# Attention: which ring of buffers keeps a wait between score matmuls and the evictions of turned queries and keys

## The chip, the cores and the metric

The kernel runs on one core of a Trainium2 chip. The metric is the device time of one execution in microseconds. PE is the matrix engine, ACT the scalar engine, DVE the vector engine, POOL the general engine, SP the engine that issues most transfers. PEld is PE's loading of weights, the operand that stays in the array. A wait is a semaphore value that an instruction's engine must see before the instruction may start; every engine takes its instructions in order, so what stands behind a waiting instruction waits too.

## What is computed

Attention with a threshold, then a feed-forward network with a squared ReLU, all of it in fp32 values (the weights of the network arrive as 64-bit floats and are converted on the chip).

```python
# q, k, v: (8, 8, 576, 64); w_in: (512, 2048); w_out: (2048, 512)
scores = q @ k.transpose(0, 1, 3, 2) / 8
scores = np.where(scores >= scores.max(-1, keepdims=True) - tau, scores, -1e9)
attn = np.exp(scores - scores.max(-1, keepdims=True))
attn = attn / (attn.sum(-1, keepdims=True) + 1e-9)
x = (attn @ v).transpose(0, 2, 1, 3).reshape(4608, 512)
h = np.maximum(x @ w_in, 0.0)
out = h * h @ w_out
```

## The kernel before

**Tiling.** Two heads of a batch element form a pair; there are 32 pairs. A pair's 576 queries are four blocks of 128 (`FULL`) and a rest of 64 (`REST`). A unit is what goes through the softmax at once: one block of 128 queries of one pair, or the two rests of two neighbouring pairs. So two pairs make nine units, eight with t < FULL and one with t = FULL, and there are 144 units. A period works on two units, A (even) and B (odd), so there are 72 periods and a few more to drain the pipeline. The unit with t = FULL is unit A of periods 4, 13, 22, ... and unit B of periods 8, 17, 26, ....

**Order.** The order of the work in a period is written out by hand, in `PLAIN`, `CONVERTING` (periods in which a chunk of the weights is converted, up to period 34) and `BEGIN_WITH`. Each name is a step: SA and SB the scores of unit A and B, T the transposes of a pair's queries or keys into PSUM (line 398), eT their eviction to SBUF by ACT (lines 403 and 411), top the maxima (DVE, line 452), pow the exponentials (ACT, line 462), mask the threshold (DVE, line 467), U, V and W the transposes of the weights of attention (lines 380 and 515), eU, eV and eW their evictions (ACT, line 523), PV the products with the values (line 532), x their eviction. `TURNS` sets the periods in which a pair's queries or keys are turned: one such turn in eight of nine periods. Query turns that matter below: pair 19 in period 39, pair 20 in period 42.

**PSUM.** One tile `sc` holds six banks. The main scores (64 x 512) of unit A are written to banks 0 and 5, those of unit B to banks 2 and 3. The small scores of both units (64 x 64, against the last 64 keys) and the turned queries and keys share banks 1 and 4. W uses banks 2 and 3, the values banks 0 and 5.

**SBUF rings.** A turned pair has three tiles (`places`, line 332): qT, the 512 queries of its full blocks, in a ring of `Q_RING` = 3 buffers; kT, its 576 keys, and qR, its 64 rest queries, in rings of `K_RING` = 4. A block unit's scores read qT and kT of its pair; the unit with t = FULL reads qR and kT of two pairs, and no qT.

**Waits.** The framework sees `sc` as one tile, and so sees a dependence between any two instructions that write and read it. `touch` (line 355) goes over the earlier instructions on other engines: where the banks are the same it adds the wait for the last of each engine, and where they are not it takes the framework's dependence away, except for the pairs of kinds in `MEET`, when the two pair numbers differ by a multiple of one of the rings given there. Those are kept, because the tiles in SBUF may be the same buffer. The kinds are "scores" (line 437) and "turned" (lines 403 and 411), with either ring.

Of the kernel before, what the change touches and what calls it, by code (L numbers as in the profile page):

```python
# [14 lines left out]
AF = mybir.ActivationFunctionType  # L15
# [33 lines left out]
def kernel(  # L49
# [25 lines left out]
    nc = tc.nc  # L75
# [5 lines left out]
    FULL = S // P  # L81
# [3 lines left out]
    BANK = 512  # L85
# [25 lines left out]
    qscale = const.tile([P, 1], FP32, name="qscale")  # L111
# [160 lines left out]
    loaded, loaded_v, turned, weights = {}, {}, {}, {}  # L272
# [59 lines left out]
    def places(i):  # L332
        if i not in turned:
            turned[i] = (
                sb.tile([P, MAIN], FP32, tag="qT", bufs=Q_RING, name="qT"),
                sb.tile([P, S], FP32, tag="kT", bufs=K_RING, name="kT"),
                sb.tile([P, REST], FP32, tag="qR", bufs=K_RING, name="qR"),
            )
        return turned[i]
# [3 lines left out]
    def ask_ahead(i, which):  # L343

        while asked[which] < min(len(pairs) - 1, i + (2 if i else 1)):
            asked[which] += 1
            (load_k if which else load_q)(asked[which])
# [2 lines left out]
    behind = mybir.DependencyInfo(mybir.DependencyClass.Sync, mybir.DependencyReason.DATA)  # L350

    Q_RING, K_RING, W_RING = 3, 4, 2
    MEET = (("scores", "turned", (Q_RING, K_RING)), ("values", "weights", (W_RING,)), ("x", "weights", (W_RING,)))

    def touch(what, made, at, size, key=0):

        if at is None:
            return
        on = range(at // BANK, (at + size - 1) // BANK + 1)
        met = {made.ins.engine}  # L360
        for kind, other, others, its in reversed(touched):
            e = other.ins.engine
            if e == made.ins.engine:
                continue
            if on[-1] < others[0] or others[-1] < on[0]:
                if any({what, kind} == {x, y} and any((key - its) % n == 0 for n in rings) for x, y, rings in MEET):
                    continue
                tc.declare_no_dep(made.ins, other.ins, reason="other banks")
            elif e not in met:
                met.add(e)  # L370
                tc.add_manual_dep(made.ins, other.ins.name, behind, reason="same bank")
        touched.append((what, made, on, key))
        while len(touched) > 300:
            touched.popleft()
# [16 lines left out]
    def turn(i, which, spots, other=None):  # L391

        nat, to = loaded.pop((i, which)), places(i)
        of = [nat[:, t, :] for t in range(FULL)] + ([loaded.pop((i, 2))] if which else [])
        for t, x in enumerate(of):
            for r, (spot, at) in enumerate(spots):
                rows = ds(r * HALF, HALF)
                made = nc.tensor.transpose(spot[:, ts(t, HALF)], x[rows, :], ident[rows, rows])  # L398
                touch("turns", made, at, BANK)
        half = FULL * HALF  # L400

        def scaled(to, spot):
            touch("turned", nc.scalar.activation(out=to, in_=spot[0], func=AF.Identity, scale=qscale[:, :]), spot[1], BANK, i)  # L403

        def then():
            part = lambda r, x, n: (spots[r][0][:, ds(x, n)], spots[r][1])
            if which:
                for r, n in ((0, half), (1, half + REST)):
                    spot = part(r, 0, n)
                    copy_by = other if r and other else nc.scalar.copy  # L410
                    touch("turned", copy_by(to[1][:, ds(r * half, n)], spot[0]), spot[1], BANK, i)
                scaled(to[2], part(0, half, REST))
                ask_ahead(i, 1)
            else:
                for r in range(2):
                    scaled(to[0][:, ds(r * half, half)], part(r, 0, half))
                ask_ahead(i, 0)

        return then
# [3 lines left out]
    def scores(n, rest):  # L423

        of, t = units[n]
        at_k, count = (MAIN, REST) if rest else (0, MAIN)
        for j in range(2):
            first = n % 2 != j
            to = (3 * j + 1) * BANK + first * (BANK - REST) if rest else (3 * j + 2 * first) * BANK
            for c in range(2):  # L430
                rows, at = ds(j * D, D), ds(c * HALF, HALF)
                qT, kT, qR = turned[of[c]]
                lhs = qT[rows, ds((c * FULL + t) * HALF, HALF)] if t < FULL else qR[rows, :]
                made = nc.tensor.matmul(  # L434
                    sc[at, ds(to, count)], lhs, kT[rows, ds(at_k, count)], start=True, stop=True
                )
                touch("scores", made, to, count, of[c])

    def softmax(n):

# [47 lines left out]
    for g in range(2, 2 * len(pairs)):  # L488
        two, x = divmod(g - 4, 4)
# [129 lines left out]
    def period(p):  # L619
# [19 lines left out]
        def turn_some():  # L639
            free = None  # L640
            if turns and p < 2:
                pq = pt_pool.tile([P, 2, BANK], FP32, tag="pt", name="pq")
                free = [(pq[:, r, :], None) for r in range(2)]
            late["turn"] = [turn(g // 2, g % 2, free or spots()) for g in turns]
# [30 lines left out]
        def scored_a():  # L675
            if has(A):
                scores(A, False)
                scores(A, True)
                scores(B_, True)
                softmax(A)  # L680
# [336 lines left out]
    with tc.manual_schedule():  # L1017
        with ExitStack() as stack:
# [18 lines left out]
            keep_busy(15)  # L1037
            pq = pt_pool.tile([P, 2, BANK], FP32, tag="pt", name="pq")
            turn(0, 0, [(pq[:, r, :], None) for r in range(2)])()
            keep_busy(8, sc[:, ds(5 * BANK, P)])  # L1040
            turn(0, 1, spots(), nc.vector.tensor_copy)()
            for i in range(1, 3):
                load_v(i)
# [88 lines left out]
        for n in range(NSTEP):  # L1132
            last = n == NSTEP - 1
# [105 lines left out]
```

## Time and profile before

| what | value |
|---|---|
| median of 3 runs | 1302.54 us (1302.05, 1302.54, 1305.91) |
| the profiled execution's own time | 1302.09 us |
| its span | 1300.3 us |
| busy PE / DVE / ACT / POOL | 1280.6 / 1009.3 / 846.5 / 916.7 us |
| attention, about 0 to 506 us | PE, DVE and ACT in turn on the chain |
| hidden layer, 506 to about 900 us | PE |
| output layer, about 900 us to the end | PE |
| line 434 (scores) on PE | 176.5 us, 2304 records |
| line 403 (scaled evictions) on ACT | 96 instructions, 0.46 us for 128x256 |

How to read it: the profile gives for each group of instructions the busy time, and the idle time of the engine just before them with what ended it. A fp32 matmul of this kernel is two or more records. The timeline merges neighbouring instructions of one line: start, length, engine, line, operation, count, and in brackets the idle time before and what ended it; the end of a matmul is modelled, so that a merged row of PE can reach a little into the next. Stretches of time are compared by the start of a line's rows.

### The profile page before, as it was taken

What the parts mean: (1) busy time and instruction counts of PE and PEld (TensorE: products, weight loads), DVE (VectorE), ACT (ScalarE), POOL (GpSimd) and SP (SyncE); (2) the same over time, 40 slices, a digit from 0 to 9 for tenths busy, and PEclk for the clock granted to TensorE, in tenths of its full rate; (3) what the DMA queues carried; (4) which work ended last, traced back from release to release, by engine and by line L of the source; (5) the groups of instructions that cost most, each with busy time, mean ns of one, the idle gap of its engine ahead of it and who ended that gap; (6) DMA issues with size and microseconds to landing.
All of it is one profiled execution on the core that took longest, in us unless ns stands there. A gap on an engine that the chain in (4) does not pass through costs nothing.

```text
span 1300.3 us, 47830 instructions
## 1 busy us (share of the span) xinstructions
PE 1280.6 (98%) x19463; PEld 1157.1 (89%) x19463; DVE 1009.3 (78%) x2431; ACT 846.5 (65%) x1498; POOL 916.7 (71%) x1023
## 2 busy tenths in 40 slices
PE   8999999999999999999999999999999999999998
PEld 5777777777777778999999999999999999999998
DVE  6999999999999995877787778777646654665463
ACT  6999999989998984757675766575523432343240
POOL 2787787755555321977897879768777767777775
PEclk9999999999999999999999999999999999999999
DMA  6656666544333312556655765579645224522411
GB/s 154 168 144 156 161 186 183 142 106 110 82 87 78 89 33 67 164 182 222 200 166 186 227 195 164 163 280 390 218 158 163 85 84 159 162 77 91 159 34 34
DMA packets 247035, 192.12 MB, mean 148 GB/s; under 512 B 97184, under 2 KB 195488, under 8 KB 246816
## 3 DMA queue, kind: packets, MB, share of 16 engines
q1 hardware_dynamic: 245504, 188.66, 48.5%
q8 instruction: 153, 2.51, 0.8%
q14 instruction: 66, 0.54, 0.1%
q10 hardware_dynamic: 1312, 0.41, 0.1%
HBM read 116.65 MB, written 72.35 MB: 145 GB/s over the span
## 4 chain that ended last, share of the span: by engine, by line
PE 91%; ACT 4%; DVE 3%; DMA 2%; issue 1%; POOL 0%; ACTq 0%; POOLq 0%; SPq 0%; DVEq 0%
PE ph L840 30%; PE po L975 29%; PE sc L532 11%; PE sc L434 10%; PE pt L380 6%; DVE arena L452 2%; PE sc L515 2%; PE sc L398 2%; ACT arena L523 1%; ACT arena L462 1%; DMA wall<-w 1%; PE sc L380 1%; DMA g<-arena 0%; ACT arena L403 0%; PE idle L1027 0%
## 5 line engine op out<-in xcount | busy, mean ns | idle before, releaser
L125 POOL TENSOR_TENSOR arena<-arena 128x512 f32<-128x512 f32 (+1 forms) x314 | 377.7, 1222 | 133.3 <-DVE arena L125 115.2
L975 PE MATMUL po<-wall,arena 128*128 128x128 f32 x3528 | 394.9, 275 | 1.4 <-ACT arena L752 1.4
L975 PEld LDWEIGHTS po<-wall,arena 128*128 128x128 f32 x3528 | 394.3, 192 | 2.0 <-ACT arena L752 1.8
L840 PE MATMUL ph<-arena,wall 128*128 128x128 f32 x3528 | 394.2, 275 | 0.7 <-DVE arena L659 0.7
L840 PEld LDWEIGHTS ph<-arena,wall 128*128 128x128 f32 x3528 | 394.0, 192 | 0.8 <-issue 0.8
L125 DVE TENSOR_TENSOR arena<-ph,arena 128x512 f32<-128x512 f32 x378 | 256.4, 689 | 86.2 <-PE ph L840 66.3
L122 POOL TENSOR_TENSOR arena<-arena 128x128 f32<-128x128 f32 (+2 forms) x314 | 254.7, 812 | 50.2 <-DMA arena<-w 33.8
L125 DVE TENSOR_TENSOR arena<-po,arena 128x128 f32<-128x128 f32 x378 | 108.3, 290 | 167.9 <-PE po L975 163.7
L467 DVE SCALAR_TENSOR_TENSOR arena<-arena 128x576 f32<-128x576 f32 x288 | 235.4, 853 | 0.7 <-ACT arena L462 0.7
L462 ACT ACTIVATE arena<-arena 128x576 f32<-128x576 f32 x288 | 208.6, 773 | 7.5 <-DVE arena L452 4.2
L452 DVE TENSOR_SCALAR_CACHE_REDUCE arena<-sc 128x576 f32<-128x576 f32 x288 | 205.2, 748 | 10.4 <-ACT arena L523 4.2
L786 ACT COPY c<-arena 128x512 f32<-128x512 f32 (+1 forms) x303 | 173.5, 579 | 50.1 <-DVE arena L122 41.3
L532 PEld LDWEIGHTS sc<-arena 64*64 64x64 f32 x5760 | 158.8, 133 | 35.6 <-DVE arena L452 19.4
L532 PE MATMUL sc<-arena 64*64 64x128 f32 (+1 forms) x5760 | 179.3, 262 | 2.7 <-DVE arena L452 1.5
L434 PE MATMUL sc<-arena 64*64 64x64 f32 (+1 forms) x2304 | 176.5, 414 | 3.4 <-ACT arena L403 2.3
L122 DVE TENSOR_TENSOR arena<-arena,c 128x512 f32<-128x512 f32 (+1 forms) x267 | 174.9, 663 | 5.9 <-ACT c L786 4.0
L523 ACT COPY arena<-pt 128x1024 f32<-128x1024 f32 x144 | 146.4, 1017 | 27.5 <-PE pt L380 26.3
L752 ACT COPY arena<-po 128x128 f32<-128x128 f32 x63 | 16.7, 264 | 186.5 <-PE po L975 183.7
L380 PEld LDWEIGHTS pt<-ident,arena 64*128 64x128 f32 x2304 | 83.4, 139 | 40.4 <-ACT arena L523 29.3
L752 ACT COPY arena<-ph 128x512 f32<-128x512 f32 x63 | 36.6, 582 | 124.3 <-PE ph L840 123.8
L434 PEld LDWEIGHTS sc<-arena 64*64 64x64 f32 x2304 | 74.2, 134 | 41.4 <-issue 14.4
L380 PE MATMUL pt<-ident,arena 64*128 64x64 f32 x2304 | 102.3, 229 | 3.6 <-ACT arena L523 2.2
(51 smaller groups left out, 918.7 us busy)
## 6 DMA issues: line engine op xcount, KB each, us to landing
g<-arena SPq DMA_DIRECT2D x144, 256.0 KB, 2.4
arena<-g SPq DMA_DIRECT2D x144, 256.0 KB, 4.6
w<-arena SPq DMA_DIRECT2D x60, 256.0 KB, 2.4
wall<-w SPq DMA_DIRECT2D x49, 256.0 KB, 5.2
arena<-w SPq DMA_DIRECT2D x44, 256.0 KB, 3.4
arena<-in_v_dram SPq DMA_DIRECT2D x32, 288.0 KB, 4.0
out_dram<-arena SPq DMA_DIRECT2D x70, 128.0 KB, 2.3
arena<-in_q_dram SPq DMA_DIRECT2D x64, 128.0 KB, 3.9
```

The lines of the kernel that those rows point to most:

```text
L122: e.tensor_tensor(out=out, in0=x, in1=y, op=ALU.subtract)
L125: e.tensor_tensor(out=out, in0=x, in1=y, op=ALU.add)
L380: made = nc.tensor.transpose(pt[:, r, ts(slot, HALF)], of[rows, :], ident[rows, rows])
L434: made = nc.tensor.matmul(sc[at, ds(to, count)], lhs, kT[rows, ds(at_k, count)], start=True, stop=True)
L452: made = nc.vector.tensor_scalar(out=s[:, j, :], in0=sc[:, ds(at, S)], scalar1=1.0, scalar2=None, op0=ALU.mult, op1=ALU.min, accum_out=nmx ...
L462: nc.scalar.activation(out=w[:, :, j, :], in_=of(j), func=AF.Exp, bias=nmx[:, j : j + 1], scale=-1.0)
L467: nc.vector.scalar_tensor_tensor(out=w[:, :, j, :], in0=of(j), scalar=thr[:, j : j + 1], in1=w[:, :, j, :], op0=ALU.is_le, op1=ALU.mult, a ...
L523: touch("weights", nc.scalar.copy(joined(to), whole(pt, 0, count)), at, 2 * BANK, m)
L532: made = nc.tensor.matmul(sc[ds(u * D, D), ds(5 * j * BANK + row, count)], loaded_v[i][rows, (c - (u != j)) % CH, :], wT[m][rows, ds(weigh ...
L786: nc.scalar.copy(c, y)
L840: nc.tensor.matmul(to[:, j, :], W_IN[m, k][:, ts(j, P)], of[k][:, m - 1, :], start=(not more and j == 0), stop=True, skip_group_check=True,)
L975: nc.tensor.matmul(to, g[:, j, :], w[:, j, :], start=(not more and j == 0), stop=(j == 3), skip_group_check=True)
```

## The change

`MEET` gets a row for each combination that shares a buffer: block scores ("scores") with queries ("q turned") in the ring of 3, block scores with keys and rest queries ("k turned") in the ring of 4, and the scores of the unit with t = FULL ("last scores") with "k turned" alone. The kind of an eviction is taken from `which` (1 for the turn of keys and rest queries), that of a score from t.

```diff
-    MEET = (("scores", "turned", (Q_RING, K_RING)), ("values", "weights", (W_RING,)), ("x", "weights", (W_RING,)))
+    MEET = (
+        ("scores", "q turned", (Q_RING,)), ("scores", "k turned", (K_RING,)), ("last scores", "k turned", (K_RING,)),
+        ("values", "weights", (W_RING,)), ("x", "weights", (W_RING,)),
+    )
...
         half = FULL * HALF
+        kind = "k turned" if which else "q turned"
...
-            touch("turned", nc.scalar.activation(out=to, in_=spot[0], func=AF.Identity, scale=qscale[:, :]), spot[1], BANK, i)
+            touch(kind, nc.scalar.activation(out=to, in_=spot[0], func=AF.Identity, scale=qscale[:, :]), spot[1], BANK, i)
...
-                    touch("turned", copy_by(to[1][:, ds(r * half, n)], spot[0]), spot[1], BANK, i)
+                    touch(kind, copy_by(to[1][:, ds(r * half, n)], spot[0]), spot[1], BANK, i)
...
-                touch("scores", made, to, count, of[c])
+                touch("scores" if t < FULL else "last scores", made, to, count, of[c])
```

## Prediction

> **What bounds the kernel now.** I read first the busy shares by stretch, to find the stage that the change touches. The columns are the stretch, its length, then the busy time and number of records of each engine, the granted clock, the DMA share and GB/s.
>
> ```profile
> 14.00:256.00 242.00, 235.32 (x5764) 175.91 (x5763) 240.12 (x647) 231.32 (x414) 185.47 (x230) 0.99 0.63 166
> 256.00:500.00 244.00, 240.16 (x6358) 181.31 (x6358) 233.83 (x704) 217.31 (x335) 118.40 (x170) 1.00 0.35 81
> 506.00:911.00 405.00, 404.44 (x3619) 404.26 (x3620) 311.00 (x493) 260.10 (x469) 320.49 (x372) 1.00 0.64 209
> ```
>
> Attention takes the first 500 us. In its first half (the weights are converted beside it) VectorE leaves 1.9 us of 242 idle and PE 6.7. In the second half PE leaves 3.8 us idle in 244 and VectorE 10.2. From 506 us on the feed-forward layers keep PE full, and no line of the change acts there. So the change is worth what it takes out of attention.
>
> Second, line 403, the eviction whose waits the change edits on ScalarE, over the whole run (us, times):
>
> ```profile
> L403 ACT ACTIVATE arena<-sc,qscale x91: 314/455/474, 7.4 to 471.2; 128x256 f32<-128x256 f32 x60, 128x64 f32<-128x64 f32 x31
> ...
> its engine sat idle before it (us, times) until:
>   DVE tau_p L119: 0.8, 1
> ```
>
> ScalarE has once stood idle before this line, for 0.8 us at the start, and never for PE. Third, line 434, the score matmuls, in the second half alone (256 to 480 us):
>
> ```profile
> L434 PE MATMUL sc<-arena x1092: 216/589/641, 255.6 to 479.7; 64*64 64x512 f32 x91, 64*64 64x64 f32 x91
> its engine sat idle before it (us, times) until:
>   ACT arena L403: 1.6, 4
> ```
>
> PE stands before the scores for line 403 four times, 1.6 us in sum, and for nothing else there. Fourth, the timeline at the first of these, PE and then ScalarE:
>
> ```profile
> 285.89 0.46 PE L515 MATMUL sc<-ident,arena 64*64 64x64 f32 x16
> 286.75 1.32 PE L434 MATMUL sc<-arena 64*64 64x512 f32 x24 [0.41 <-ACT arena L403]
> 288.00 0.52 PE L398 MATMUL sc<-ident,arena 64*128 64x64 f32 x10
> ...
> 285.89 0.81 ACT L403 ACTIVATE arena<-sc,qscale 128x256 f32<-128x256 f32 x2
> 286.60 1.00 ACT L523 COPY arena<-pt 128x1024 f32<-128x1024 f32 x1
> ```
>
> The scores start 0.05 us after the second eviction ends (285.89 + 0.81 = 286.70). The same picture, with 0.41, 0.41 and 0.42 us, stands at 345.90, 405.02 and 464.45.
>
> **The change, part by part.** The instructions of both programs, engine by engine, are the same ones in the same order; eleven waits differ.
>
> (a) Seven query evictions (line 403, periods 8, 17, 26, 35, 44, 53, 62) no longer wait for the last of the 64-row score matmuls. Cost and gain 0: by the second view ScalarE never stood there for PE. In those periods powers (line 462) lie before the eviction on ScalarE, and each waits for a maximum that reads the same group's scores. If that cover were gone, at most one 64x512 pass (0.59 us by the median of the mixed row above) would show per site, 4 us in all, and that would be a gain. I take 0, because the row that measures it shows none.
>
> (b) At the four sites above (periods 40, 49, 58, 67) the four main matmuls of the 64-row unit lose their wait for the query evictions. There the unit's first pair and the evicted pair differ by 3 (pair 16 and pair 19), which is a hit in the ring of 3, though these matmuls read no tile of that ring. The third small matmul of the group now waits for the second eviction, the first for the first one: they write the banks that the evictions read, so these waits are real.
>
> What a site is worth I take from a period that has the same evictions and not the wait, period 43, ahead of which pair 20's queries are evicted (that unit belongs to pair 19, which differs by 1):
>
> ```profile
> 306.00 0.46 PE L515 MATMUL sc<-ident,arena 64*64 64x64 f32 x16
> 306.28 1.27 PE L434 MATMUL sc<-arena 64*64 64x512 f32 x24
> 307.48 0.53 PE L398 MATMUL sc<-ident,arena 64*128 64x64 f32 x10
> ...
> 305.77 0.82 ACT L403 ACTIVATE arena<-sc,qscale 128x256 f32<-128x256 f32 x2
> ```
>
> From the start of line 515: scores at +0.28, transposes (line 398) at +1.48, and, further on in that timeline, the next filling of pt at +1.84, the second scores at +2.44, the values at +3.35, the next line 515 at +6.52 (312.52). At the site: +0.86, +2.11, +2.48, +3.07, +3.98, +7.15 (293.04). From the transposes on the difference is 0.63 us at every step. It is larger than the idle 0.41 because the first scores overlap the tail of line 515 when they need not wait (0.17 us more), and the group itself is 0.05 shorter. So a site is worth 0.63 us, bounded from below by the idle alone, 0.41, and from above by the 0.72 us that VectorE idles there (below).
>
> Is the wait only moved to the small matmuls? If the main ones start at 285.89 + 0.28 = 286.17, they run 0.91 us (the second scores of the period before, 281.87, to the values, 282.78), to 287.08. The second eviction has ended at 286.70. Cover 0.38 us; the two new waits cost 0, and in period 43 the weight loads show a wait of 0.28 us for line 403 in this very place and PE none. Without the cover they would cost the whole gain.
>
> What is late next, with everything 0.63 us earlier, at the first site: the filling of pt would come at 287.74, and the copy that frees it (line 523) ends at 287.60: 0.14 us left. The second scores at 288.33 need the copy of the middle banks, which ends at 288.09: 0.24 left. VectorE's first maximum:
>
> ```profile
> 288.65 0.76 DVE L452 TENSOR_SCALAR_CACHE_REDUCE arena<-sc 128x576 f32<-128x576 f32 x1 [0.72 <-ACT arena L523]
> ```
>
> It stands 0.72 us behind the mask before it, which ends at 287.92. The copy named had ended at 288.09, so the last to come is PE's transposes in the same bank (288.00 + 0.52). Moved to 288.02 it keeps 0.1 us of idle. All later steps hang on these, so the 0.63 us is carried on. POOL waits 2.6 us each period for VectorE and has no backlog there.
>
> One wait fewer on the first matmul also takes away an extra instruction of PE's queue:
>
> ```profile
> L434 PEldq EVENT_SEMAPHORE  x1: 51/51/51, 285.9 to 285.9; - x1
> ```
>
> It lies in the idle before 286.75 and is worth 0 by itself. The Trainium skill (Perfetto Trace Analysis, "Identifying Dependency Chains") says that an instruction that waits for several engines may get EventSemaphore instructions ahead of it; the trace agrees, and counted as a gain of its own that would be 4 x 0.051 = 0.2 us more, a time of 1299.8.
>
> The sum: 4 x 0.63 = 2.5 us. The profiled execution took 1302.09 with a span of 1300.3: the span becomes 1297.8, that execution 1299.6. It lies 0.45 us under the median of the runs shown (1302.54), so I forecast 1302.54 - 2.5 = **1300.0**, 0.19% less. Own range: 4 x 0.41 = 1.6 gives 1300.9, 4 x 0.72 = 2.9 gives 1299.7, widened to 1298.5 to 1301.5 for the scatter of a median (the two lower runs lie 0.5 us apart, the highest 3.4 above them).
>
> **The rivals.** *Absorbed* (1302.5): VectorE is 96% busy in the second half (233.83 of 244), so PE's time could be off the path that sets the end. Against it: VectorE idles 0.71 to 0.72 us at all four sites, right behind PE's stall, and the period behind the first site makes up at most 0.2 us of the stall (6.34 us from line 515 to line 515, 293.04 to 299.38, in a period that turns nothing; period 43 took 6.52 and turns keys). It also covers the change not doing what it says, the stall coming back at the small matmuls (cover 0.38).
>
> *More* (1290.6 to 1295.3): weight loads before line 434 wait 11.6 us for line 403 in 256 to 480, 29 times. Four of them (0.55 each, 2.2 us) are the sites; if the other 9.4 us were false waits as well and all on the path, the time would be 1302.5 - 2.5 - 9.4 = 1290.6; half of it on the path gives 1295.3. Against it: the programs differ in no other wait, and PE stands at none of the 25.
>
> *Slower* (1305.2): behind the hidden layer the chain runs through one queue of transfers, four in a row at 890 to 911 us.
>
> ```profile
> 896.21 5.07 DMA wall<-w
> 901.35 5.15 DMA g<-arena
> ```
>
> If the shift put one more store (5.15 us) ahead of a weight's reload there, it would cost 5.2 - 2.5 = 2.7 us over before. It decides only if a transfer of that stage is timed by something other than the stage itself. Against it: these loads and stores are issued behind semaphores of the same stage, which starts 2.5 us earlier as a whole.
>
> **How the numbers follow.** Forecast 79%, absorbed 12%, more 5%, slower 4%. I call 0.3% (3.9 us) what a measurement of this kernel can tell from no change: faster means under 1298.6. Forecast and absorbed lie inside it but for the scatter of a median: 10 points of the forecast's 79 may fall under 1298.6. Faster 0.05 + 0.10 = 0.15; slower 0.04; same 0.81. The range 1297.8 to 1302.8 takes in the forecast's own range, the absorbed case and some of the scatter; it leaves out the case of more, the slower one, and about 5 points of scatter.
>
> **What would show it.** In the profile after: no PE wait for line 403 before the scores between 256 and 480 us; at each site line 515 to the transposes 1.48 us in place of 2.11; VectorE's 0.72 us before the first maximum down to about 0.1; the feed-forward part starts at 503.5 in place of 506.0 and takes as long as before; the first half ends where it did. It is wrong if the scores start early and the transposes don't, if the period behind a site grows by what was won, or if the start of the feed-forward part moves by under 1.6 or over 2.9 us.

## The result and the profile after

Over 13 executions each the changed kernel took 1301.14 us (median, 1298.72 to 1304.56), the kernel before 1303.27 us (1301.62 to 1305.91). The ratio is 0.9983, 95% interval [0.9975, 0.9991]: 0.17% faster, some 2.2 us, and so less than the 0.3% set out above. The profiled execution has a span of 1298.3 us against 1300.3.

The first view again, busy time by stretch, of the changed kernel (stretch, its length, PE, PEld, DVE, ACT, POOL, granted clock, DMA share, GB/s):

```profile
14.00:256.00 242.00, 234.83 (x5760) 175.94 (x5763) 239.71 (x647) 230.47 (x414) 184.37 (x230) 0.99 0.63 166
256.00:500.00 244.00, 241.37 (x6406) 182.61 (x6398) 234.81 (x708) 218.61 (x336) 119.06 (x170) 1.00 0.35 80
506.00:911.00 405.00, 404.45 (x3622) 404.26 (x3621) 312.80 (x497) 260.21 (x470) 322.64 (x374) 1.00 0.64 210
```

In the second half of attention PE's idle time falls from 3.8 to 2.6 us, in a stretch of the same length that now holds more of the work. The other two rows stand nearly as they did. The scaled evictions (line 407 now) on ACT, over the whole run, and the scores (line 438) on PE, from 256 to 480 us:

```profile
L407 ACT ACTIVATE arena<-sc,qscale x91: 309/455/482, 7.2 to 469.2; 128x256 f32<-128x256 f32 x60, 128x64 f32<-128x64 f32 x31
...
its engine sat idle before it (us, times) until:
  DVE tau_p L119: 0.7, 1
```

```profile
L438 PE MATMUL sc<-arena x1096: 216/589/641, 255.7 to 477.7; 64*64 64x512 f32 x92, 64*64 64x64 f32 x91
its engine sat idle before it (us, times) until:
```

Nothing stands under the scores' "sat idle" any more; the four waits of 1.6 us are gone. So are the four extra instructions (EVENT_SEMAPHORE) that stood ahead of these scores. The timeline at the first site, PE, then ACT, then DVE:

```profile
286.40 0.46 PE L519 MATMUL sc<-ident,arena 64*64 64x64 f32 x16
286.68 1.27 PE L438 MATMUL sc<-arena 64*64 64x512 f32 x24
287.88 0.53 PE L401 MATMUL sc<-ident,arena 64*128 64x64 f32 x10
```

```profile
286.41 0.82 ACT L407 ACTIVATE arena<-sc,qscale 128x256 f32<-128x256 f32 x2
```

```profile
288.37 0.08 DVE L471 DVE_READ_ACCUMULATOR arena<-arena 128x1 f32 x1
288.53 0.76 DVE L456 TENSOR_SCALAR_CACHE_REDUCE arena<-sc 128x576 f32<-128x576 f32 x1
```

The scores start 0.28 us behind line 519 (line 515 of before), while the evictions still run, and the transposes 1.48 us behind it, in place of 2.11. VectorE's gap ahead of its first maximum is 0.08 us (288.45 to 288.53), in place of 0.72.

From the rows of line 515 or 519, period to period, the whole gain can be followed. "Moved" is the changed kernel's start less that of before, in these two profiles. A period's length runs from the row of the period before it to its own row:

| period | before | moved | length before | length after |
|---|---|---|---|---|
| 27 | 202.65 | -0.06 | 7.09 | 7.08 |
| 34 | 252.66 | +0.52 | 6.89 | 6.89 |
| 39 | 285.89 | +0.51 | 6.45 | 6.45 |
| 40 (site) | 293.04 | -0.12 | 7.15 | 6.52 |
| 48 | 345.02 | -0.14 | 6.44 | 6.44 |
| 49 (site) | 352.18 | -0.79 | 7.16 | 6.51 |
| 58 (site) | 411.31 | -1.43 | 7.15 | 6.51 |
| 67 (site) | 470.72 | -2.01 | 7.15 | 6.51 |
| 72 | 501.14 | -2.01 | 4.78 | 4.78 |

Four steps of 0.63, 0.65, 0.64 and 0.64 make 2.56 us. The feed-forward part then starts at 504.00 in place of 506.01 and takes 794.3 us in both. The 0.58 us lost between periods 27 and 34 goes against the change, in a stretch where no wait is altered (those of ScalarE stand in periods 26 and 35); experiments 2, 4 and 8 bear on it.

### The profile page after: what moved, and what is told of

The parts are those of the page before. It is cut to its first block, busy times and chain, and to the rows that moved or that the text cites. A ratio compares the mean times of both kernels' runs of the same rounds, so it can differ in the third digit from the quotient of the medians.

```text
span 1298.3 us, 47826 instructions
## 1 busy us (share of the span) xinstructions
PE 1279.7 (99%) x19463; PEld 1157.1 (89%) x19463; DVE 1009.6 (78%) x2431; ACT 845.8 (65%) x1498; POOL 916.8 (71%) x1023
## 4 chain that ended last, share of the span: by engine, by line
PE 93%; DVE 3%; ACT 2%; DMA 1%; issue 1%; POOL 0%; ACTq 0%; POOLq 0%; SPq 0%; DVEq 0%
PE ph L844 30%; PE po L979 29%; PE sc L536 12%; PE sc L438 10%; PE pt L383 6%; DVE arena L456 2%; PE sc L519 2%; PE sc L401 2%; ACT arena L527 1%; PE sc L383 1%; DMA wall<-w 1%; ACT arena L466 1%; DMA g<-arena 0%; PE idle L1031 0%; ACT arena L415 0%
```

## The experiments

Each is compared with runs of the kernel before on the same chip. The length of a period runs, as above, from the row of line 515 (519 or 522 where the edit moves lines) of the period before it to its own.

### 1 and 2: one engine's waits alone

The added rows keep the old waits, for evictions (1, so that only PE's waits change) or for scores (2, so that only ScalarE's do).

```diff
+    OLD = tuple((s_, t_, (Q_RING, K_RING)) for s_ in ("scores", "last scores") for t_ in ("q turned", "k turned"))
...
-                if any({what, kind} == {x, y} and any((key - its) % n == 0 for n in rings) for x, y, rings in MEET):
+                meet = MEET + OLD if what.endswith("turned") else MEET    # 1; in 2: what.endswith("scores")
+                if any({what, kind} == {x, y} and any((key - its) % n == 0 for n in rings) for x, y, rings in meet):
```

PE's alone:

> Only the four waits of PE (periods 40, 49, 58, 67) are changed; the seven waits of ScalarE stay as before. Theory (the whole gain is PE's, 0.63 us at a site): from line 515's row to the transposes 1.48 us at all four sites, line 515 to line 515 6.51 there in place of 7.15, time 2.5 us under before, ratio 0.998. Rival (the seven evictions matter too): less than the full change, ratio above 0.9985, and ScalarE shows idle before the scaled evictions for PE.

Measured: 1299.97 us (8 runs) against 1302.99, ratio 0.9974 [0.9964, 0.9985]. The forecast of 0.998 lies inside. All four sites have 6.51 or 6.52 us.

ScalarE's alone:

> Only the seven waits of ScalarE are changed; the four of PE stay. Theory: nothing, ratio 1.000 within 0.001, the four sites at 2.11 us from line 515 to the transposes as before, and period to period within 0.05 us of before in quiet stretches. Rival (earlier evictions help, or disturb the first half, where the changed kernel lost 0.5 us between 203 and 246 us): a period behind 8, 17 or 26 differs by over 0.1 us, ratio away from 1 by over 0.001.

Measured: 1302.69 us (11 runs), ratio 0.9996 [0.9988, 1.0005]. The sites keep 7.14 to 7.16 us, and the periods behind 8, 17 and 26 agree with before to 0.02 us (7.08, 7.07 and 7.09 against 7.09, 7.07 and 7.09). The scores of experiment 2 on PE, 256 to 480 us, show the four waits as before:

```profile
L441 PE MATMUL sc<-arena x1092: 213/589/641, 255.7 to 480.3; 64*64 64x512 f32 x91, 64*64 64x64 f32 x91
its engine sat idle before it (us, times) until:
  ACT arena L410: 1.6, 4
```

So the four waits of PE alone give a gain whose interval overlaps that of the whole change, and the seven of ScalarE alone none that the runs can tell from zero. That the first gain looks larger than the whole (0.26% against 0.17%) is not shown to be more than scatter; the sites gain the same in both.

### 3: the wait at fifteen sites

```diff
+    ALL = tuple((s_, "q turned", (1,)) for s_ in ("scores", "last scores"))
...
+                meet = MEET + ALL if what.endswith("scores") else MEET
```

> The changed kernel, but the scores of every unit wait for the query evictions ahead of them, as at the four sites before: 15 sites in the second half in place of 4 (before) or 0 (changed). Theory: each site costs 0.63 us, so 15 x 0.63 = 9.5 us over the changed kernel and 11 x 0.63 = 6.9 us over before, ratio to before 1.0053. Rival (a stall is partly made up where VectorE has no idle): under 0.4 us a site, under 4.4 us over before.

Measured: 1307.72 us (5 runs), ratio to before 1.0035 [1.0022, 1.0048], that is 4.6 us (2.9 to 6.3). The 6.9 us of the theory lie outside. The stall is there at the sites, but it doesn't have one price. Periods 40, 49, 58 and 67 cost 0.64 again; 36, 43, 52 and 61 cost 0.40 to 0.42, periods 38, 47 and 56 0.50 or 0.51, and 45, 54 and 63 0.62 to 0.64. The fifteenth site, period 65, has a length that scatters without the wait too (below). Two of the cheaper sites and a dear one in this kernel's timeline, PE and the evictions:

```profile
306.52 0.46 PE L522 MATMUL sc<-ident,arena 64*64 64x64 f32 x16
307.17 1.32 PE L441 MATMUL sc<-arena 64*64 64x512 f32 x24 [0.18 <-ACT arena L410]
319.89 0.46 PE L522 MATMUL sc<-ident,arena 64*64 64x64 f32 x16
320.76 1.32 PE L441 MATMUL sc<-arena 64*64 64x512 f32 x24 [0.41 <-ACT arena L410]
333.63 0.46 PE L522 MATMUL sc<-ident,arena 64*64 64x64 f32 x16
334.37 1.32 PE L441 MATMUL sc<-arena 64*64 64x512 f32 x24 [0.28 <-ACT arena L410]
```

```profile
306.30 0.82 ACT L410 ACTIVATE arena<-sc,qscale 128x256 f32<-128x256 f32 x2
319.89 0.81 ACT L410 ACTIVATE arena<-sc,qscale 128x256 f32<-128x256 f32 x2
333.50 0.81 ACT L410 ACTIVATE arena<-sc,qscale 128x256 f32<-128x256 f32 x2
```

The evictions start 0.22, 0.00 and 0.13 us before line 522; they end 0.60, 0.81 and 0.68 us behind its start, and 0.05 to 0.06 us later the scores start, at +0.65, +0.87 and +0.74. Less the +0.28 of scores that need not wait, and with 0.05 for the longer group, that makes 0.42, 0.64 and 0.51. The price of the wait is how far the second eviction ends behind the point at which PE would be ready. The rival that a stall is partly made up later is not needed for the smaller sum: the periods between sites keep the lengths that they have in the changed kernel, to 0.01 us.

### 4 and 8: the same two kernels once more

> The kernel before, once more, for the scatter of its stages. If the 0.5 us that the changed kernel lost between 203 and 246 us is scatter of that stretch, this profile shows line 515's rows there moved by some tenths of a us against the first profile of the same kernel, while 256 to 470 us repeats to 0.05 us. If it belongs to the change, this profile repeats the first one to 0.1 us there too.

> The changed kernel once more. Theory: the second half repeats to 0.05 us (line 515 to line 515 6.51 at the four sites), and all difference of the span comes from the first 250 us, where profiles of one kernel lay up to 1.9 us apart.

| profile | granted clock, 10 to 30 us | first row of line 515/519 | second row | period 34 | 35 to 72, without 65 | feed-forward starts | span |
|---|---|---|---|---|---|---|---|
| before | 0.91 | 18.11 | 26.02 | 252.66 | 234.50 | 506.01 | 1300.3 |
| before again | 0.83 | 19.06 | 27.89 | 254.56 | 234.49 | 507.72 | 1301.8 |
| changed | 0.91 | 17.95 | 25.86 | 253.18 | 231.94 | 504.00 | 1298.3 |
| changed again | 0.91 | 17.94 | 25.91 | 251.63 | 231.90 | 502.61 | 1297.5 |

The start of period 34 scatters within one kernel by 1.90 us (before) and 1.55 us (changed). The two have different origins. Of the 1.90 us, 1.87 are there by the second row, at 26 us, and they go with the clock granted to PE: in the ten profiles of this case the second row lies at 24.59 and 24.84 us where the clock from 10 to 30 us was 1.00 (experiments 5 and 1), at 25.74 to 26.24 where it was 0.91 (seven profiles), and at 27.89 where it was 0.83. The 1.55 us arise at the same clock, in periods 3, 11, 13 and 28 to 32; their cause is open. Between 203 and 246 us the distance of the two profiles of before changes by 0.5 us (from 1.64 to 2.15), and that of the two of the changed kernel by 1.1 (from 0.47 to 1.56). The 0.58 us that the changed kernel lost there is therefore of the size of the scatter, and "changed again" has nothing of it.

The second half, without the one period (65) that scatters there too (6.64 to 7.04 us in these four), repeats to 0.04 us and differs between the kernels by 2.55 to 2.60. Two things were not foreseen: period 65, and that the feed-forward part differs as well, by 0.8 us in these four profiles (794.1 to 794.9 us).

### 5: the small matmuls ahead of the main ones

```diff
             if has(A):
-                scores(A, False)
                 scores(A, True)
                 scores(B_, True)
+                scores(A, False)
```

> The changed kernel with the order within the first score step turned round: the eight small matmuls (banks 1 and 4, which wait for the evictions whatever the ring) ahead of the four main ones. Theory (the main matmuls, 0.91 us, cover those waits): the cover is gone, the small ones stall as the main ones did before, by 0.3 to 0.6 us in the 15 periods of the second half behind a query eviction and by about 0.6 us in the 15 behind a key eviction (there the last eviction ends at +0.83 from line 515's start, against scores at +0.28), 11 to 18 us over the changed kernel in all; the small waits show as PE idle before the scores for the evictions. Rival (the small matmuls have no wait worth a cover): the time of the changed kernel within 1 us.

Measured: 1315.69 us (4 runs), ratio to before 1.0089 [1.0073, 1.0106], 11.6 us over before and, with 0.9983 for the changed kernel, some 14 us over that one. From period 35 to 72 it takes 15.7 us longer. Periods behind a query eviction grow by 0.41 to 0.44 or by 0.56 to 0.59 (period 65 apart), those behind a key eviction by 0.64 to 0.67, but for four of them with 0.35 to 0.38, and the one in nine that follows no turn by 0. The scores on PE, 256 to 500 us, and two of their rows, behind a key and behind a query eviction:

```profile
L438 PE MATMUL sc<-arena x1124: 218/589/641, 255.7 to 499.6; 64*64 64x512 f32 x95, 64*64 64x64 f32 x93
its engine sat idle before it (us, times) until:
  ACT arena L407: 6.4, 15
...
267.70 1.32 PE L438 MATMUL sc<-arena 64*64 64x64 f32 x24 [0.42 <-ACT arena L407]
274.37 1.67 PE L438 MATMUL sc<-arena 64*64 64x64 f32 x24
```

The fifteen idle times are those of the key evictions, whose last instruction (the rest queries, 64 columns) is of line 407 too. Behind a query eviction no idle time is shown: there the stall lies inside the row, 1.67 us long in place of 1.27. The four cheap periods (41, 50, 59, 68) turn nothing; in the changed kernel PE stands 0.24 us there for the copy that frees pt, at 294.71 in period 41, and in this run it doesn't. The new stall takes the place of that one, and only the rest is paid.

So the small matmuls' waits are real and need a cover, and the main matmuls give it, 0.91 us long.

### 6 and 7: more work for PE, in each half

```diff
             if has(A):
-                scores(A, False)
+                for _ in range(2 if p in range(10, 25) else 1):    # 7: range(42, 57)
+                    scores(A, False)
```

> The changed kernel; in the 15 periods 10 to 24 (first half) the four main matmuls of unit A are made twice, the second time with the same result: 0.91 us more of PE a period. Theory (in the first half VectorE sets the pace and PE has little room, 6.7 us in 242): some of it is absorbed, periods 10 to 24 grow by 0.2 to 0.9 us each, 3 to 13 us in all. Rival (PE is the path there too, so that the same false wait would have cost the same in the first half): 15 x 0.91 = 13.7 us. Rival (VectorE alone is the path): 0.

> The same 0.91 us more of PE in the 15 periods 42 to 56 of the second half. Theory (PE sets the pace there, so a stall of PE is paid in full): 15 x 0.91 = 13.7 us over the changed kernel. Rival of the prediction (absorbed, since VectorE is 96% busy there): under 7 us.

Measured in the second half (7): 1313.80 us (4 runs), ratio 1.0077 [1.0062, 1.0092], and with 0.9983 for the changed kernel some 12 us over that one; the 15 periods grow by 13.2 us in the profile, ten of them by 0.84 to 0.87, which is about the length that the second set adds to the row of scores (2.13 in place of 1.27), three by 0.55 to 0.79 and two by 1.27 and 1.30. In the first half (6): 1307.61 us (8 runs), ratio 1.0028 [1.0018, 1.0039], some 6 us over the changed kernel; the 15 periods grow by 7.9 us, 0.53 on average, but unevenly, from -0.05 to 0.97. The busy time of the changed kernel and of experiment 6 from 80 to 180 us, in this order:

```profile
80.00:180.00 100.00, 98.16 (x2450) 73.56 (x2450) 99.93 (x269) 96.07 (x172) 80.34 (x100) 1.00 0.62 162
```

```profile
80.00:180.00 100.00, 99.72 (x2363) 74.89 (x2367) 94.17 (x252) 87.91 (x162) 75.46 (x93) 1.00 0.58 151
```

In the first half VectorE is the full engine (99.93 of 100), and with the added matmuls PE takes its place while VectorE falls to 94.17. About 0.4 of the 0.9 us a period are absorbed. PE's idle time, 1.84 us in these 100, is too small to hold them. Most of what is absorbed comes out of the matmuls with the values (line 536): over the 15 periods their same 1224 records are busy for 38.5 us in the changed kernel and 34.1 in experiment 6. They counted as busy and yet could be shorter; what drew them out, the profile does not say. In the second half nearly all of the added time is paid, so "absorbed" falls there.

## Why the prediction was right

**The sum.** Four sites at 0.63 us each were forecast and 0.63 to 0.65 came (2.56 in place of 2.52). The control was well chosen: at the sites the changed kernel shows the steps of period 43, +0.28, +1.48 and 6.51 or 6.52 to the next line 515. The idle time that the profile gives, 0.41, would have been a third too low. The extra instruction on PE's queue (0.051 us) was rightly put at nothing: it is gone at all four sites, and they gained 0.63 to 0.65 with it.

**The seven waits of ScalarE at nothing.** Shown by experiment 2, with an interval of 0.12% below to 0.05% above.

**The wait is not moved to the small matmuls.** PE shows no idle before the scores after the change, and experiment 5 shows what the cover of the main matmuls is worth.

**What is late next.** The margin of 0.1 us before VectorE's first maximum was 0.08; the copy that frees pt ended at 288.12 (287.12 + 1.00) and the next filling started at 288.24, 0.12 us later against 0.14 reckoned. Nothing took the wait's place.

**Absorbed.** Experiment 7 shows that added time of PE is paid nearly in full in this half (13.2 us in the profile, of the 13.7 expected). What the prediction had for it, VectorE's gap right behind PE's, was the right sign. **More.** The weight loads ahead of the scores still wait 10.6 us for the evictions, 29 times, and PE stands at none of them; experiment 5 shows what such waits cost without a cover. **Slower.** The feed-forward part took 794.3 us before and after (794.1 and 794.9 in the repeated profiles), so it shows nothing of the 5.15 us of a store.

**What was off.** The start of the feed-forward part was forecast at 503.5 and came at 504.00, because the first half was supposed to repeat, and it doesn't to better than 1.9 us. The time of 1300.0 was forecast from a median of 3 runs, 1302.54; over 13 runs the kernel before has 1303.27 and the changed one 1301.14. The scatter of such a median goes in part with the granted clock: the changed kernel's four executions at 0.999 have a median of 1299.94 us, its seven at 0.997 one of 1301.81. That 1301.14 lies in the range says little by itself, for the absorbed case lay in it too; the interval of the ratio leaves out no change, and the rows of the four sites and experiments 1, 2 and 7 show where the gain comes from. And the value of 0.63 us holds for these four sites alone: experiment 3's expectation carried it to eleven others and was too high by half, because the eviction ends earlier there, as period 43's own rows (eviction 0.23 us before line 515) already showed.

## What to carry to other kernels

The idle time ahead of a waiting instruction is not the whole price of the wait: look for a place in the same trace that has the same work without the wait, and subtract row from row (here 0.63 against 0.41). A wait costs what its releaser ends behind the point at which the waiting engine is ready, so one and the same false wait is worth a different sum in each place, and less where another wait of the same engine follows that would have held it anyway (experiment 5, 0.35 to 0.38 in place of about 0.65). Where a real wait must stay, put independent work of the same engine ahead of it; here 0.91 us of it a period was worth some 14 us of the kernel's time.

## What was not expected

The second half of attention repeats from profile to profile to 0.04 us over 234 us, with one period apart, while the start of period 34 scatters by up to 1.9 us. In the two profiles of before nearly all of that is there after 26 us, with a different granted clock; in the two of the changed kernel, at the same clock, it arises later. A change of 2 us is then far clearer in the rows of its own stage than in the time of the kernel. And in a stage where VectorE is busy 99.93 us of 100, more work on PE still cost more than half of its length (0.53 of about 0.9 us a period).
